# Sums of two matmuls side by side in 27 steps of two halves instead of 28

## The chip, the cores and the metric

The kernel runs on one NeuronCore of a Trainium2 chip. The metric is the device time of one execution in microseconds (us). The engines are TensorE (PE, with its weight loads as PEld), VectorE (DVE), ScalarE (ACT), GpSimd (POOL) and SyncE (SP); here nearly all transfers are issued from SP's queue.

## The reference

A transformer block on `x` of 2048 rows and 576 columns, all float32. Six vectors `sa, ca, ga, sb, cb, gb` come from `silu(c) @ w_mod`.

```python
h = layernorm(x) * (1 + ca) + sa
q, k, v = split(h @ wqkv)                 # 32 heads of 18
p = softmax(q @ k.T * 18 ** -0.5)
x = x + ga * ((p @ v) @ wo)
h = layernorm(x) * (1 + cb) + sb
x = x + gb * (silu(h @ w1) @ w2)          # w1: 576 x 4608, w2: 4608 x 576
```

## The kernel before

To keep float32 accuracy with a rounded matmul type, most operands are split into a high and a low part, and a product is the sum of high x high, high x low and low x high. The 576 columns are four tiles of 128 and a fifth of 64. `PASS` lists 14 passes of a sum: three for each of the four full tiles, and two for the fifth. The fifth tile has its 64 columns twice: rows 0 to 63 hold the high part of the activation, rows 64 to 127 its low part, and the weights stand on both halves alike. So one pass with the high weights gives high x high and low x high, and a second with the low weights gives high x low and, on the lower half, low x low.

Work comes in quads of four heads by a block of 512 queries: four blocks of eight quads. A quad has a stage of score maxima (`psa`, L674, reduced by DVE at L676), then the exponential scores (`psb`, L731, ACT at L733) and the value sums (`psv`, L768, four matmuls of 32 columns for each key tile). The maxima of a finished quad are negated and split into `ms` (`max_a`), transposed (`pst`), copied to `mt` (`max_copy`), and written by four small transfers (`max_rows`, L710) into spare rows of the queries `qt`; the exponential scores of that quad need them.

When the eight quads of a block are done, `post` queues its output projection (`proj`, `psp`), layernorm, transpositions (`o_T`, `h_T`) and the feed-forward network (`mlp1`, the first layer, and `mlp2`) as pieces of a filler, which are spread between the score steps of the next block. What is left after the fourth block runs alone: the tail (`state["tail"]`). `Pair` carries out two sums at once. Outside the tail it works in halves of 64 rows: in one step one matmul on rows 0 to 63 and one on rows 64 to 127 run side by side for the two sums, which change places half way, at step 14:

```python
for h in (1, 0) if late else (0, 1):
    g = 1 - h if late else h
```

A pair of 14 passes is thus 28 steps. `GR` and `GP` cut these steps into parts for the filler. In the tail a step is one matmul on all 128 rows.

PE runs in the order in which the program issues. That order is set by a planner (`Plan`, `Filler`), which adds up costs of parts (`MMC`, `MMH`) and chooses at each turn between a score step ("half"), a run of value sums ("values") and a piece of filler ("half", or "full" for transpositions and other matmuls of 128 rows). The other engines' queues are ordered by a scheduler from the program's dependencies and buffers.

During the first block's projection and network the weights are converted (`weights`): a half of a tile is loaded into a staging buffer `raw` (three buffers), POOL multiplies it by the gate where there is one (L826), copies the high part (L827) and subtracts for the low part (L828), and the tile is stored for the later blocks (L829).

Of the kernel before, what the change touches and what calls it, by code (L numbers as in the profile page):

```python
# [18 lines left out]
P = 128  # L19
# [42 lines left out]
PB = 7  # L62
QKB = 3
GS = 2
GR = [range(i, min(i + GS, 28)) for i in range(0, 28, GS)]
NG = len(GR)
GQ = (range(0, 4), range(4, 8), range(8, 11), range(11, 14))
G2 = [range(i, i + 3) for i in range(0, 24, 3)]
GP = [range(i, i + 2) for i in range(0, 28, 2)]
MMC = 231  # L70
MMH = 133

# [260 lines left out]
def tile_adaln_block(ctx: ExitStack, tc: tile.TileContext, x, wqkv, wo, w1, w2, c, wfirst, wcol, out):  # L333
# [114 lines left out]
    class Pair:  # L448
# [3 lines left out]

        def __init__(self, ps, ops, n, halves, planned=True):
            self.ps, self.ops, self.n, self.halves, self.planned = ps, ops, n, halves, planned
            if planned:
                self.release = [plan.take("f") for _ in ps]

        def step(self, s):  # L460
            late, i = divmod(s, self.n)
            if not self.halves:
                lhsT, rhs = self.ops(late, i)
                mm(self.ps[late], lhsT=lhsT, rhs=rhs, start=(i == 0), stop=(i == self.n - 1))  # L464
                return
            for h in (1, 0) if late else (0, 1):
                g = 1 - h if late else h
                lhsT, rhs = self.ops(g, i)
                rows = slice(64 * h, 64 * h + 64)
                done = mm(self.ps[g], lhsT=lhsT[rows], rhs=rhs[rows], start=(s == 0), stop=(s == 2 * self.n - 1))  # L470
                if h == 1 and s == self.n - 1:
                    self.last = done
                    if self.planned:
                        self.change()
                        half["at"] = None
                        plan.op("A", plan.t + 200, 20, lambda t: half.update(at=t + TR))
                elif h == 1 and s == self.n:
                    tc.add_manual_dep(done.ins, self.turn.ins.name, SYNC, reason="the other halves' writes to this bank")
# [208 lines left out]
            later.append((now + MB, 3, 110, lambda: max_b(t), lambda: t.get("ms_at")))  # L687

    def max_a(t):
        negm = at1.tile([P, 4, NST], F32, name="negm", bufs=2)  # L690
        nc.vector.tensor_reduce(negm, t["mx"], axis=AX.X, op=ALU.max, negate=True)
        ms = at1.tile([P, 2, 4, NST], F32R, name="ms", bufs=2)
        nc.vector.tensor_copy(ms[:, 0], negm)
        nc.vector.tensor_sub(ms[:, 1], negm, f(ms[:, 0]))
        t["ms"] = ms
        chain([("V", 230), ("V", 180), ("V", 180)], plan.t, None, lambda at: t.update(ms_at=at + TR))
# [4 lines left out]
        return ps  # L701

    def max_copy(t, ps):
        t["mt"] = at1.tile([32, P], F32R, name="mt", bufs=2)
        nc.vector.tensor_copy(t["mt"], ps[:32, :P])

    def max_rows(t):
# [69 lines left out]
    def out_b(i, ov):  # L777
        b, qd = divmod(i, NQUAD)
        ps = aux([P, NST, P], "pso")
        for s4 in range(NST):  # L780
            nc.tensor.transpose(ps[:, s4, :], ov[:, s4 * P:(s4 + 1) * P], ident)  # L781
        rec = att.tile([P, NST, 4], F32, name="rec", bufs=2)
        psr = ps.rearrange("p s (h c) -> p s h c", h=4)
        nc.vector.reciprocal(rec, psr[:, :, :, DH])
        if qd == 0:
            if b:
                fill.until("h_T")
            o[b] = att.tile([P, NST, 640], F32, tag="o", name="ot", bufs=1)
        for s4 in range(NST):
            nc.vector.tensor_mul(o[b][:, s4, 72 * qd:72 * qd + 72].rearrange("p (h c) -> p h c", h=4), psr[:, s4, :, :DH],  # L790
                                 rec[:, s4, :, None].to_broadcast([P, 4, DH]))
        rel = plan.take("a")
        chain([("V", 260)] + [("V", 225)] * 4, plan.t + 100, None, rel)
        del quads[i]
        if qd == NQUAD - 1:
            nc.gpsimd.tensor_copy(o[b][:, :, D:640], o[b][:, :, 512:D])
            post(b)
# [18 lines left out]
    def weights(w, src, scr, first, gate=None):  # L816

        if not first:
            nc.sync.dma_start(f(w), f(scr))
            return  # L820
        n = w.shape[2] // 2
        for cs in (slice(0, n), slice(n, 2 * n)):
            raw = mp["p"].tile([P, 320], F32, tag="raw", name="raw", bufs=3)[:, :n]
            nc.sync.dma_start(raw, src[:, cs])
            if gate is not None:
                nc.gpsimd.tensor_tensor(raw, raw, gate[:, cs], op=ALU.mult)  # L826
            nc.gpsimd.tensor_copy(w[:, 1, cs], raw)  # L827
            nc.gpsimd.tensor_tensor(w[:, 0, cs], raw, f(w[:, 1, cs]), op=ALU.subtract)  # L828
        nc.sync.dma_start(f(scr), f(w))  # L829
# [16 lines left out]
    def post(b):  # L846
# [7 lines left out]

        def o_T(kt):
            if kt == 0:
                c["th"] = pool.tile([P, KT, QB], F32R, tag="th", name="th")
                c["tl"] = pool.tile([P, 4, QB], F32R, tag="tl", name="tl")
            ps = bank("psT", psF)
            for j in range(NST):  # L860
                nc.tensor.transpose(ps[:, j * P:(j + 1) * P], ob[:, j, kt * P:(kt + 1) * P], ident)
            hi = c["th"][:, kt, :]
            chain([("A", 600), ("V", 690)], plan.t, None, plan.take("f"))
            nc.scalar.activation(hi, ps, AF.Copy)
            if kt < 4:
                nc.vector.tensor_sub(c["tl"][:, kt, :], ps, f(hi))
            else:
                nc.vector.tensor_sub(hi[64:], ps[64:], f(hi)[64:])

        def proj(j, part):  # L870
            if part == 0:
                def ops(g, i):
                    kt, a, w = PASS[i]
                    return (c["tl"] if a else c["th"])[:, kt, j * P:(j + 1) * P], c["wo", kt][:, 1 - w, g * HH:(g + 1) * HH]

                c["pp"] = Pair([bank("psp", psA)[:, :HH] for _ in range(2)], ops, 14, not state["tail"])
            for s in GP[part]:
                c["pp"].step(s)
            if part == len(GP) - 1:
                for g in range(2):  # L880
                    add_x1(j, g, c["pp"].ps[g])
                    plan.op("AV"[g == 0], plan.t + 200, 440, c["pp"].release[g])
# [19 lines left out]

        def h_T(kt):
            if kt == 0:
                c["hh"] = pool.tile([P, KT, QB], F32R, tag="th", name="hh")
                c["hl"] = pool.tile([P, 4, QB], F32R, tag="tl", name="hl")
            ps = bank("psT", psF)
            chain([("A", 780), ("V", 430)], plan.t, plan.take("f"))
            for j in range(NST):
                nc.tensor.transpose(ps[:, j * P:(j + 1) * P], ob[:, j, kt * P:(kt + 1) * P], ident)  # L910
            tmp, hi = etmp(), c["hh"][:, kt, :]
            mod_out(ps, kt, 1, tmp)
            mod_hi(hi, tmp)
            mod_lo(kt, hi, c["hl"][:, kt, :] if kt < 4 else None, tmp, nc.vector if last and kt % 2 == 0 else nc.gpsimd)

        def rest(n):
# [44 lines left out]
        def mlp1(i, part):  # L961
            if part == 0:
                def ops(g, k):
                    kt, a, w = PASS[k]
                    return c["w1", i + g][:, 1 - w, kt * P:(kt + 1) * P], (c["hl"] if a else c["hh"])[:, kt, :]

                c["p1"] = Pair([bank("ps1", psA) for _ in range(2)], ops, 14, not state["tail"])
            for s in GR[part]:
                c["p1"].step(s)
            if part < NG - 1:  # L970
                return
            us = c["p1"].ps
            if not state["tail"]:

                us = [etmp(), etmp()]
                nc.scalar.activation(us[0], c["p1"].ps[0], AF.Copy)
                nc.vector.tensor_copy(us[1], c["p1"].ps[1])
                for n in range(2):
                    chain([(("A", 600), ("V", 690))[n], ("A", 630), ("V", 690), ("A", 630)], plan.t + 200, c["p1"].release[n])
            for g_ in range(2):  # L980
                u, t = us[g_], etmp()
                nc.scalar.activation(t, u, AF.Tanh, scale=0.5)  # L982
                nc.vector.scalar_tensor_tensor(t, t, 1.0, u, op0=ALU.add, op1=ALU.mult)  # L983
                g = pool.tile([P, 2, QB], F32R, tag="g", name="g", bufs=GB)
                nc.scalar.activation(g[:, 0, :], t, AF.Copy)  # L985
                (nc.vector if last else nc.gpsimd).tensor_tensor(g[:, 1, :], t, f(g[:, 0, :]), op=ALU.subtract)  # L986
                c["g", i + g_] = g
# [565 lines left out]
```

## Time and profile before

| | |
|---|---|
| median of 3 runs | 2488.92 us (2485.57 to 2490.62) |
| profiled execution | 2492.01 us, span 2490.2 us |
| granted TensorE clock | 0.996 |
| busy: PE, DVE, ACT, POOL | 96%, 72%, 60%, 23% |
| first-layer matmuls of 64 rows, on `hh` and on `hl` | 2160 and 864 records, some missing |
| projection matmuls of 64 rows, on `th` and on `tl` | 480 and 192 |

A row of the timeline gives start, length, engine, line, operation, output and inputs, and a count; in brackets stands how long the engine was idle before it and what ended that. L470 is `Pair`'s matmul in halves, L464 the one on all rows. A matmul's length includes its way through the array, so matmuls that follow each other overlap in the records; what one costs is read from start to start.

### The profile page before, as it was taken

Reading aid. Unit: us, or ns where it says so; the run is one execution under the profiler, and the core shown is the slowest. Engines: PE = TensorE matmul, PEld = TensorE weight load, DVE = VectorE, ACT = ScalarE, POOL = GpSimd, SP = SyncE. Lnnn points to the kernel's source line nnn. Section 1 sums busy time; section 2 is a strip of 40 time slices with the busy share of each in tenths; the row PEclk is TensorE's granted clock in tenths of the full one; section 3 lists DMA queues with packets and bytes.
Section 4 is the critical chain, followed back from the end, with each engine's and each line's share of the span. In section 5 each row is a group of like instructions: output and inputs, shape, how many; then the busy total and the mean of one; then the engine's idle time right before and its main releaser. Section 6 shows DMA issues by size and latency. Waiting matters only on the chain.

```text
span 2490.2 us, 51321 instructions
## 1 busy us (share of the span) xinstructions
PE 2399.7 (96%) x20192; PEld 1574.5 (63%) x20192; DVE 1787.7 (72%) x3180; ACT 1490.4 (60%) x2712; POOL 577.9 (23%) x729
## 2 busy tenths in 40 slices
PE   5999999998999999999999999999999999999999
PEld 4874344433556666666666666666666666678988
DVE  7868788887877777777877777778777777334333
ACT  4237667766666766666666666666666666742121
POOL 4100000012566566652211111111211111110000
PEclk9999999999999999999999999999999999999999
DMA  6843333343455555553543433332633343226563
GB/s 234 269 133 110 110 108 110 110 146 106 137 180 184 169 181 179 199 168 123 172 146 128 144 125 127 131 134 95 209 127 121 127 160 118 103 101 239 172 221 120
DMA packets 159394, 372.02 MB, mean 149 GB/s; under 512 B 17754, under 2 KB 55034, under 8 KB 159154
## 3 DMA queue, kind: packets, MB, share of 16 engines
q1 hardware_dynamic: 154562, 366.45, 44.1%
q8 instruction: 160, 2.62, 0.5%
q10 hardware_dynamic: 4592, 2.29, 0.3%
q14 instruction: 80, 0.66, 0.1%
HBM read 282.35 MB, written 85.80 MB: 148 GB/s over the span
## 4 chain that ended last, share of the span: by engine, by line
PE 86%; DVE 7%; DMA 2%; ACT 2%; POOL 1%; issue 1%; SPq 1%; ACTq 0%; DVEq 0%; POOLq 0%
PE ps L470 26%; PE psv L768 19%; PE psa L674 14%; PE ps L464 10%; PE psb L731 8%; DVE mx L676 4%; PE psqk L551 3%; PE psp L470 1%; PE psv L470 1%; PE pso L781 1%; DVE etmp L983 1%; DMA xt<-in_x 1%; PE psp L464 1%; ACT pt L733 1%; ACT etmp L982 1%
## 5 line engine op out<-in xcount | busy, mean ns | idle before, releaser
L676 DVE TENSOR_REDUCE mx<-psa 128x1 f32<-128x512 f32 x2048 | 1345.4, 687 | 372.5 <-PE psb L731 250.1
L733 ACT ACTIVATE pt<-psb 128x512 f32<-128x512 f32 x2048 | 1163.1, 598 | 562.2 <-PE psb L731 393.3
L674 PE MATMUL psa<-kt,qt 54*128 54x512 f32 x2048 | 770.4, 424 | 26.9 <-DVE mx L676 22.7
L731 PE MATMUL psb<-qt,kt 56*128 56x512 f32 x2048 | 787.8, 428 | 8.5 <-DMA qt<-mt 5.1
L674 PEld LDWEIGHTS psa<-kt,qt 54*128 54x128 f32 x2048 | 345.6, 185 | 418.2 <-DVE mx L676 279.7
L768 PE MATMUL psv<-pt,vt 128*32 128x512 f32 x4096 | 534.7, 605 | 0.0
L470 PE MATMUL ps<-w2t,g 64*128 64x288 f32 x4992 | 417.5, 294 | 0.1
L470 PEld LDWEIGHTS ps<-w2t,g 64*128 64x128 f32 x4992 | 387.0, 186 | 35.2 <-issue 10.6
L470 PE MATMUL ps<-hh,w1t 64*128 64x512 f32 x2160 | 384.6, 395 | 1.7 <-POOL hh L405 1.6
L731 PEld LDWEIGHTS psb<-qt,kt 56*128 56x128 f32 x2048 | 347.3, 185 | 39.1 <-ACT pt L733 18.4
L470 PEld LDWEIGHTS ps<-hh,w1t 64*128 64x128 f32 x2160 | 219.8, 186 | 60.5 <-issue 10.6
L986 POOL TENSOR_TENSOR g<-etmp,g 128x512 fp32r<-128x512 f32 x108 | 138.3, 1297 | 405.4 <-ACT g L985 345.4
L891 POOL TENSOR_TENSOR x<-x,gt 128x288 f32<-128x288 f32 x116 | 92.8, 800 | 489.1 <-ACT gt L890 479.1
L768 PEld LDWEIGHTS psv<-pt,vt 128*32 128x32 f32 x4096 | 93.6, 108 | 177.7 <-issue 169.2
L470 PE MATMUL ps<-hl,w1t 64*128 64x512 f32 x864 | 185.7, 393 | 1.0 <-POOL hl L403 1.0
L887 DVE TENSOR_TENSOR x<-ps,x 128x288 f32<-128x288 f32 x184 | 84.0, 457 | 122.6 <-PE ps L464 71.5
L464 PE MATMUL ps<-w2t,g 128*128 128x288 f32 x960 | 130.6, 295 | 1.7 <-ACT g L985 0.9
L464 PEld LDWEIGHTS ps<-w2t,g 128*128 128x128 f32 x960 | 128.6, 188 | 3.3 <-ACT g L985 1.2
L982 ACT ACTIVATE eq<-ps 128x512 f32<-128x512 f32 x36 | 21.6, 599 | 146.3 <-PE ps L464 146.3
L464 PE MATMUL ps<-hh,w1t 128*128 128x512 f32 x360 | 106.8, 390 | 0.5 <-DVE hh L405 0.5
L529 POOL TENSOR_TENSOR wql<-raw,wqh 128x640 fp32r<-128x640 f32 x13 | 20.7, 1589 | 372.6 <-PE psa L674 112.0
L470 PEld LDWEIGHTS ps<-hl,w1t 64*128 64x128 f32 x864 | 93.0, 186 | 18.5 <-POOL hl L403 2.8
(140 smaller groups left out, 2084.7 us busy)
## 6 DMA issues: line engine op xcount, KB each, us to landing
w1t<-w1s SPq DMA_DIRECT2D x108, 640.0 KB
w2t<-w2s SPq DMA_DIRECT2D x108, 576.0 KB
kt<-kscr SPq DMA_DIRECT2D x512, 108.0 KB
w1s<-w1t SPq DMA_DIRECT2D x36, 640.0 KB
w2s<-w2t SPq DMA_DIRECT2D x36, 576.0 KB
vt<-vscr SPq DMA_DIRECT2D x32, 608.0 KB
qt<-qscr SPq DMA_DIRECT2D x128, 108.0 KB
raw<-in_w SPq DMA_DIRECT2D x72, 160.0 KB
```

The costliest lines, as they stand in the source:

```text
L464: mm(self.ps[late], lhsT=lhsT, rhs=rhs, start=(i == 0), stop=(i == self.n - 1))
L470: done = mm(self.ps[g], lhsT=lhsT[rows], rhs=rhs[rows], start=(s == 0), stop=(s == 2 * self.n - 1))
L551: mm(qk_ps[0], lhsT=w[b][:, kt, :], rhs=(hTl if a else hTh)[:, kt, n * 512:(n + 1) * 512], start=(i == 0), stop=(i == 13))
L674: mm(ps, lhsT=t["q"][64 * j:64 * j + 54, hp, stt * P:(stt + 1) * P], rhs=t["k", kc, hp][64 * j:64 * j + 54, :], start=True, stop=True)
L676: return lambda: nc.vector.tensor_reduce(t["mx"][:, 2 * j + hp, stt, kc:kc + 1], ps, axis=AX.X, op=ALU.max)
L731: mm(ps, lhsT=t["k", kt // 4, hp][64 * e:64 * e + 56, kt % 4 * P:(kt % 4 + 1) * P], rhs=t["q"][64 * e:64 * e + 56, hp, :], start=True, sto ...
L733: nc.scalar.activation(t["P"][kt, hp][:, e, :], ps, AF.Exp, scale=SCALE)
L768: mm(t["ps"][32 * h:32 * h + 32, :], lhsT=t["v"][:, c0:c0 + 32], rhs=t["P"][kt, h // 2][:, h % 2, :], start=(kt == 0), stop=(kt == NKT - 1 ...
L887: nc.vector.tensor_add(c["x1"][j][:, hs], ps, c["x1"][j][:, hs])
L891: nc.gpsimd.tensor_add(c["x1"][j][:, hs], c["x1"][j][:, hs], t)
L982: nc.scalar.activation(t, u, AF.Tanh, scale=0.5)
L986: (nc.vector if last else nc.gpsimd).tensor_tensor(g[:, 1, :], t, f(g[:, 0, :]), op=ALU.subtract)
```

## The change

The low x low product is left out. The high part of the fifth tile is copied by ACT to rows 64 to 127 of an extra column block (index `KT`) of `th` and `hh`. The second sum's high x low product of the fifth tile then runs on these rows at step 13, beside the first sum's; step 27 falls away for both sums. This holds for `proj` and `mlp1` outside the tail. `GP` and `GR` have 14 parts as before, the last one of one step, and the planner is given the smaller cost. The copies are also made in the tail, where nothing reads them. For the space of the extra columns, `raw` has two buffers instead of three, and `negm`, `ms`, `mt` and `rec` one instead of two.

```diff
-GR = [range(i, min(i + GS, 28)) for i in range(0, 28, GS)]
+GR = [range(i, min(i + GS, 27)) for i in range(0, 27, GS)]
-GP = [range(i, i + 2) for i in range(0, 28, 2)]
+GP = [range(i, min(i + 2, 27)) for i in range(0, 27, 2)]
...
+        def half(self, g, h, i):
+            if self.extra and g == 1 and h == 1 and i == self.n - 1:
+                lhsT, rhs = self.extra()
+            else:
+                lhsT, rhs = self.ops(g, i)
+            rows = slice(64 * h, 64 * h + 64)
+            return lhsT[rows], rhs[rows]
...
+            end = 2 * self.n - (2 if self.extra else 1)
             for h in (1, 0) if late else (0, 1):
                 g = 1 - h if late else h
-                lhsT, rhs = self.ops(g, i)
-                rows = slice(64 * h, 64 * h + 64)
-                done = mm(self.ps[g], lhsT=lhsT[rows], rhs=rhs[rows], start=(s == 0), stop=(s == 2 * self.n - 1))
+                lhsT, rhs = self.half(g, h, i)
+                done = mm(self.ps[g], lhsT=lhsT, rhs=rhs, start=(s == 0), stop=(s == end))
...
-        negm = at1.tile([P, 4, NST], F32, name="negm", bufs=2)
+        negm = at1.tile([P, 4, NST], F32, name="negm", bufs=1)
-        ms = at1.tile([P, 2, 4, NST], F32R, name="ms", bufs=2)
+        ms = at1.tile([P, 2, 4, NST], F32R, name="ms", bufs=1)
-        t["mt"] = at1.tile([32, P], F32R, name="mt", bufs=2)
+        t["mt"] = at1.tile([32, P], F32R, name="mt", bufs=1)
-        rec = att.tile([P, NST, 4], F32, name="rec", bufs=2)
+        rec = att.tile([P, NST, 4], F32, name="rec", bufs=1)
-            raw = mp["p"].tile([P, 320], F32, tag="raw", name="raw", bufs=3)[:, :n]
+            raw = mp["p"].tile([P, 320], F32, tag="raw", name="raw", bufs=2)[:, :n]
...
-                c["th"] = pool.tile([P, KT, QB], F32R, tag="th", name="th")
+                c["th"] = pool.tile([P, KT + 1, QB], F32R, tag="th", name="th")
+                nc.scalar.activation(c["th"][64:, KT, :], ps[64:], AF.Copy)
                 nc.vector.tensor_sub(hi[64:], ps[64:], f(hi)[64:])
...
+                def extra():
+                    return c["th"][:, KT, j * P:(j + 1) * P], c["wo", 4][:, 0, HH:2 * HH]
-            for s in GP[part]:
+            for s in range(28)[2 * part:2 * part + 2] if state["tail"] else GP[part]:
...
-                c["hh"] = pool.tile([P, KT, QB], F32R, tag="th", name="hh")
+                c["hh"] = pool.tile([P, KT + 1, QB], F32R, tag="th", name="hh")
+            if kt == 4:
+                nc.scalar.activation(c["hh"][64:, KT, :], tmp[64:], AF.Copy)
...
+                def extra():
+                    return c["w1", i + 1][:, 0, 4 * P:5 * P], c["hh"][:, KT, :]
-            for s in GR[part]:
+            for s in range(28)[GS * part:GS * part + GS] if state["tail"] else GR[part]:
```

Three places show how the change moves instructions. Up to the first projection the order on PE is the same in both kernels.

The first is on PE, the second half of the first projection pair. `wo` with a number is a tile of the weights, 6314 the fifth; two matmuls make a step. First the kernel before, then the changed one:

```order
L470 MATMUL psp<-wo_6290,th 128x288 x4
L470 MATMUL psp<-wo_6290,tl 128x288 x2
L470 MATMUL psp<-wo_6302,th 128x288 x2
L674 MATMUL psa<-kt_86,qt 128x512
L731 MATMUL psb<-qt,kt_90 128x512
L470 MATMUL psp<-wo_6302,th 128x288 x2
L470 MATMUL psp<-wo_6302,tl 128x288 x2
L470 MATMUL psp<-wo_6314,th 128x288 x4
```

```order
L480 MATMUL psp<-wo_6290,th 128x288 x4
L480 MATMUL psp<-wo_6290,tl 128x288 x2
L480 MATMUL psp<-wo_6302,th 128x288 x4
L480 MATMUL psp<-wo_6302,tl 128x288 x2
L480 MATMUL psp<-wo_6314,th 128x288 x2
L684 MATMUL psa<-kt_86,qt 128x512
L741 MATMUL psb<-qt,kt_90 128x512
```

The fifth tile has one step instead of two, and the score step in between has moved behind the pair.

The second is on PE in the last block of attention, where the outputs of a finished quad are transposed (`pso`). Before, then changed:

```order
L470 MATMUL ps_25030<-w2t,g 128x288
L470 MATMUL ps_25031<-w2t,g 128x288
L781 MATMUL pso<-ident,ov 128x128 x4
L768 MATMUL psv_25116<-pt_2108,vt_2109 32x512 x2
L768 MATMUL psv_25116<-pt_2102,vt_2109 32x512 x2
L768 MATMUL psv_25116<-pt_2103,vt_2109 32x512 x2
L768 MATMUL psv_25116<-pt_2104,vt_2109 32x512 x2
L674 MATMUL psa<-kt_88,qt 128x512
```

```order
L778 MATMUL psv_24873<-pt_2105,vt_2109 32x512 x2
L778 MATMUL psv_24873<-pt_2106,vt_2109 32x512 x2
L684 MATMUL psa<-kt_89,qt 128x512
L741 MATMUL psb<-qt,kt_92 128x512
L684 MATMUL psa<-kt_89,qt 128x512
L741 MATMUL psb<-qt,kt_93 128x512
L791 MATMUL pso<-ident,ov 128x128 x4
L480 MATMUL ps_25012<-w2t,g 128x288
L480 MATMUL ps_25013<-w2t,g 128x288
```

Before, the transposition was followed by a run of value sums; now score steps stand between the value run and the transposition, and steps in halves follow it.

The third is on SP in the first block's network, ahead of the maxima's transfers of a quad (`qt<-mt`). `raw` loads bring weights, `w1s` and `w2s` store them. Before, then changed:

```order
L829 DMA w1s<-w1t 128x1280
L824 DMA raw<-in_w 128x288
L648 DMA kt_87<-kscr 54x512
L824 DMA raw<-in_w 128x288
L829 DMA w1s<-w1t 128x1280
L824 DMA raw<-in_w 128x288
L710 DMA qt<-mt 1x8x128 x4
```

```order
L658 DMA kt_87<-kscr 54x512
L839 DMA w2s<-w2t 128x1152
L834 DMA raw<-in_w 128x320 x2
L839 DMA w1s<-w1t 128x1280
L834 DMA raw<-in_w 128x320
L834 DMA raw<-in_w 128x288
L720 DMA qt<-mt 1x8x128 x4
```

Other weights stand ahead of the maxima's transfers than before, and the key load has moved ahead of them.

More of the change, by code (lines that the diff above doesn't have):

```diff
@@ L448, in tile_adaln_block, with __init__ @@
     class Pair:
-        def __init__(self, ps, ops, n, halves, planned=True):
-            self.ps, self.ops, self.n, self.halves, self.planned = ps, ops, n, halves, planned
+        def __init__(self, ps, ops, n, halves, planned=True, extra=None):
+            self.ps, self.ops, self.n, self.halves, self.planned, self.extra = ps, ops, n, halves, planned, extra
             if planned:
                 self.release = [plan.take("f") for _ in ps]
+        def half(self, g, h, i):
[5 more added lines that the diff above has]
+            return lhsT[rows], rhs[rows]
         def step(self, s):
@@ L874, in ops @@
                     return (c["tl"] if a else c["th"])[:, kt, j * P:(j + 1) * P], c["wo", kt][:, 1 - w, g * HH:(g + 1) * HH]
-                c["pp"] = Pair([bank("psp", psA)[:, :HH] for _ in range(2)], ops, 14, not state["tail"])
-            for s in GP[part]:
+                def extra():
+                    return c["th"][:, KT, j * P:(j + 1) * P], c["wo", 4][:, 0, HH:2 * HH]
+                c["pp"] = Pair([bank("psp", psA)[:, :HH] for _ in range(2)], ops, 14, not state["tail"], extra=None if state["tail"] else extra)
+            for s in range(28)[2 * part:2 * part + 2] if state["tail"] else GP[part]:
                 c["pp"].step(s)
@@ L965, in ops @@
                     return c["w1", i + g][:, 1 - w, kt * P:(kt + 1) * P], (c["hl"] if a else c["hh"])[:, kt, :]
-                c["p1"] = Pair([bank("ps1", psA) for _ in range(2)], ops, 14, not state["tail"])
-            for s in GR[part]:
+                def extra():
+                    return c["w1", i + 1][:, 0, 4 * P:5 * P], c["hh"][:, KT, :]
+                c["p1"] = Pair([bank("ps1", psA) for _ in range(2)], ops, 14, not state["tail"], extra=None if state["tail"] else extra)
+            for s in range(28)[GS * part:GS * part + GS] if state["tail"] else GR[part]:
                 c["p1"].step(s)
```

## The prediction

> **What bounds the kernel now.** I read the page's busy shares and chain first, then busy time by stage, then what TensorE waits for while the feed-forward network runs, and last the timeline of TensorE there. The stage rows give start and end, length, and busy time (instructions) of PE, PEld, DVE, ACT and POOL, then granted clock, DMA share and GB/s. The stages are cut at the first transposition after each attention block (562 us is just before the first one's end).
>
> ```profile
> PE 2399.7 (96%) x20192; PEld 1574.5 (63%) x20192; DVE 1787.7 (72%) x3180; ACT 1490.4 (60%) x2712; POOL 577.9 (23%) x729
> PE 86%; DVE 7%; DMA 2%; ACT 2%; POOL 1%; issue 1%; SPq 1%; ACTq 0%; DVEq 0%; POOLq 0%
> ...
> 562.00:657.00 95.00, 81.60 (x631) 40.40 (x626) 77.19 (x154) 58.30 (x105) 25.86 (x44) 0.98 0.30 94
> 657.00:1214.00 557.00, 540.93 (x5098) 357.49 (x5098) 427.43 (x730) 368.18 (x665) 313.95 (x433) 1.00 0.53 171
> 1214.00:1752.00 538.00, 532.42 (x5092) 355.91 (x5090) 415.98 (x726) 365.42 (x661) 88.20 (x90) 1.00 0.41 138
> 1752.00:2249.00 497.00, 492.11 (x4542) 335.11 (x4541) 321.68 (x574) 318.92 (x583) 82.57 (x82) 1.00 0.38 131
> ```
>
> From 657 to 2249 us TensorE is busy for 1565.5 of 1592 us (98%) at full clock, and 86% of the chain is its own work. A busy share can hide waits under overlapping matmuls, so the waits of PE's own queue in that stretch (total us, times, longest):
>
> ```profile
> PE psa L674 <- DVE mx L676: 8.0, 15, 1.0
> PE psb L731 <- DMA qt<-mt: 3.9, 1, 3.9
> PE pst L700 <- DVE mx L676: 2.8, 5, 0.6
> ```
>
> The largest is 8.0 us in 1592. So there a step of TensorE that is left out should come off the end, unless something else takes its place. Now the price of a step, of a run of value sums (L768), and of going in and out of it, from the timeline of PE (start, length, line, operation, count):
>
> ```profile
> 1402.80 0.39 PE L674 MATMUL psa<-kt,qt 54*128 54x512 f32 x1
> ...
> 1403.12 0.28 PE L700 MATMUL pst<-ident,ms 128*32 128x128 f32 x1
> 1403.33 0.73 PE L470 MATMUL ps<-hh,w1t 64*128 64x512 f32 x4
> 1403.90 0.39 PE L470 MATMUL ps<-hl,w1t 64*128 64x512 f32 x2
> ...
> 1405.75 0.39 PE L674 MATMUL psa<-kt,qt 54*128 54x512 f32 x1
> ...
> 1406.07 1.07 PE L768 MATMUL psv<-pt,vt 128*32 128x512 f32 x8
> 1407.07 0.49 PE L674 MATMUL psa<-kt,qt 54*128 54x512 f32 x1
> ...
> 1407.41 0.62 PE L470 MATMUL ps<-hh,w1t 64*128 64x512 f32 x4
> ...
> 1411.37 0.63 PE L470 MATMUL ps<-hh,w1t 64*128 64x512 f32 x4
> 1411.93 1.92 PE L768 MATMUL psv<-pt,vt 128*32 128x512 f32 x16
> 1413.79 0.50 PE L674 MATMUL psa<-kt,qt 54*128 54x512 f32 x1
> ```
>
> Lengths overlap, so I take starts. Between 1407.41 and 1411.37 stand 17 steps of two halves (first-layer and score steps cost alike): 3.96 / 17 = 0.233 us a step. A value run of one key tile (x8) takes 1.00 us to the next start, of two (x16) 1.86: 0.86 a tile and 0.14 fixed. Going in costs 1406.07 - 1405.75 = 0.32 against 0.233, +0.09; the first step after it 1407.41 - 1407.07 = 0.34, +0.11. A full-row transposition costs +0.09 on the way in (1403.12 - 1402.80 = 0.32) and +0.10 behind it (0.57 for two steps).
>
> **The change part by part.**
>
> Steps removed, the gain. A first-layer pair gives up one step of 0.233. Blocks one to three each have 18 such pairs, 54 x 0.233 = 12.6 us. The order of the instructions agrees: 108 first-layer matmuls fewer. A projection pair is shorter (288 columns):
>
> ```profile
> 1176.66 0.43 PE L470 MATMUL psp<-wo,th 64*128 64x288 f32 x4
> ...
> 1177.45 0.41 PE L731 MATMUL psb<-qt,kt 56*128 56x512 f32 x1
> ```
>
> Six steps lie between these starts, 0.79 / 6 = 0.132 us; 4 pairs in 3 blocks give 12 x 0.132 = 1.6 us. The fourth block (the tail) keeps 28 full-row steps. Together -14.2 us, all in the stretch where TensorE waits for next to nothing. The Trainium skill (TensorE: Matmul & The Clock Gate, Back-to-back issue gap) gives 216 ns between warm matmuls of 512 columns, N/2.4 + 2.5 ns. By that the two terms would be 54 x 0.216 + 12 x 0.1225 = 13.1 us, an estimate from the page; the trace's 0.233 decides.
>
> The new order, a loss. Costs of parts set the order that the planner writes for PE, so everything behind the first projection moves. I counted in the two orders how often PE changes its kind of work from there to the end of attention: half-row to values 269 before and 288 after, values to half-row 291 and 300, half-row to full 65 and 62, full to half-row 43 and 50, full to values 24 and 14; 293 value runs become 302. At the prices above: 19 x 0.09 = 1.7; 9 x (0.14 + 0.11) = 2.2; -3 x 0.09 = -0.3; 7 x 0.10 = 0.7; full to values no row above prices alone, so -10 x (0 to 0.10), I take 0.05 as the middle, -0.5. Sum +3.9 us. Bounds: 0, if these drains lie beside waits that would have been there anyway, to 4.4. I take 3.9, since the waits are so few.
>
> The new copies on ScalarE: 8, one in each projection's and one in each first layer's transpositions, 64 x 512. Nearest row, same columns:
>
> ```profile
> L864 ACT ACTIVATE th<-psT x20: 578/598/637, 603.7 to 2221.4; 128x512 fp32r<-128x512 f32 x20
> ...
> ACT pt L733 <- PE psb L731: 304.0, 418, 4.4
> ```
>
> Median 598 ns, so 4.8 us of ACT work in all. From 560 to 2220 us ACT stands idle 304 us waiting for scores from PE (second row), which covers it; I take 0. Without that cover each of the six before the tail would hold up the exponentials queued behind it by 0.6 us, and those hold up score banks: at most 3.6 us. The low end is 0, since a copy added can shorten nothing. The planner does not count these copies. In the tail ACT is idle for most of the time, 48.00 us busy of 241 by the stage row,
>
> ```profile
> 2249.00:2490.00 241.00, 233.61 (x1392) 211.48 (x1391) 89.80 (x158) 48.00 (x77) 3.03 (x4) 1.00 0.54 189
> ```
>
> so 0 there too. The waits for the half-way turn stay where they were (step 14).
>
> Maxima rings and the reciprocals' ring of one instead of two: the next write of such a tile now waits for the last reader of the quad before. The last of these readers, `qt<-mt`, must leave before the quad's exponential scores start, and the next write is a quad later (successive maxima):
>
> ```profile
> 850.77 0.22 DVE L691 TENSOR_REDUCE negm<-mx 128x16 f32<-128x64 f32 x1
> 917.16 0.22 DVE L691 TENSOR_REDUCE negm<-mx 128x16 f32<-128x64 f32 x1
> ```
>
> 66 us apart, so 0. Were a read ever that late, VectorE would stand with the score maxima queued behind it.
>
> Raw staging of two instead of three. This matters only while the first block converts weights (up to about 1150 us). A load into `raw` waits, on SP's queue, until POOL is done with the tile that had the buffer; behind it on SP stand key loads and the four small `qt<-mt` transfers, without which a quad's exponential scores cannot start. Even with three buffers this bit once:
>
> ```profile
> 717.73 0.77 SPq L648 DMA_DIRECT2D kt<-kscr  x1
> 723.45 0.33 SPq L824 DMA_DIRECT2D raw<-in_w  x1
> 725.04 0.32 SPq L829 DMA_DIRECT2D w1s<-w1t  x1
> 725.46 0.38 SPq L824 DMA_DIRECT2D raw<-in_w  x1
> 725.93 2.84 SPq L710 DMA_DIRECT2D qt<-mt  x4
> ...
> 719.62 0.27 DVE L705 CAST mt<-pst 32x128 fp32r<-32x128 f32 x1
> ...
> 722.16 0.44 POOL L827 CAST w1t<-raw 128x320 fp32r<-128x320 f32 x1
> 722.57 0.86 POOL L828 TENSOR_TENSOR w1t<-raw,w1t 128x320 fp32r<-128x320 f32 x1
> ...
> 730.06 0.47 PE L731 MATMUL psb<-qt,kt 56*128 56x512 f32 x1 [3.89 <-DMA qt<-mt]
> ```
>
> The maxima were ready at 719.9 (719.62 + 0.27). SP had stood since 718.5 before a `raw` load that went out at 723.45, when POOL's subtraction at 722.57 had freed its buffer; the maxima left at 725.93, and PE stood 3.89 us. That is one of the eight quads that meet such a queue. With two buffers each load waits on a nearer reader, so the same can strike more often: bounds 0 (the scheduler that orders SP has pushed loads apart, and no PE row names a late weight) and 8 x 3.9 = 31 us. I take half a stall more, 2 us, nearest to the one in eight that the trace shows. That the weights themselves come late I take as 0: POOL is busy 313.95 of 557 us in that stage.
>
> Sum: -14.2 + 3.9 + 2 = -8.3 us. The profiled execution took 2492.0 (span 2490.2), which gives 2483.7. It lies 3.1 us above the median of the runs, 2488.9, so against the median 2480.6: I say 2481.
>
> **The rivals.**
>
> *VectorE becomes the bound, about 2489.* Each score bank is released by a maximum on DVE. In 562 to 657 us DVE is 81% busy (77.19 of 95) and PE only 86%; in the blocks behind, DVE is at 77% (427.43 of 557; 415.98 of 538). Taking 4.7 us of PE work out of a block raises that to 78%. If PE waits for banks by what it saves, the block keeps its length and the time is that of before. Against it: of all PE waits in these blocks only 8.0 us were for these maxima. The Trainium skill (TensorEngine Tiling (Array Packing), PSUM Bottleneck) says that tiling speeds TensorE and not the emptying of PSUM, which may then bind; by that rule this rival would hold, and the trace's 8.0 us speak against it so far.
>
> *SP's queue makes it slower, 2494 or more.* Place: `qt<-mt` behind `raw` loads in the first block. With -14.2 + 3.9 the change has 10.3 us to lose; four stalls of 3.9 more (15.6 us) put it 5.3 above, 2494.2; all eight quads 2510. It decides from four further stalls on. For it: the row at 730.06, and the new order has six transfers of weights just ahead of `qt<-mt` at that quad. Against: seven of eight quads went free.
>
> *The changes of mode cost nothing, 2475.* If the extra value runs stand where PE would have waited anyway, and no stall comes, the whole 14.2 arrives: 2488.9 - 14.2 = 2474.7. Against it are the dense starts above. That the step is not really left out is no rival: the order has 132 matmuls fewer.
>
> **How the numbers follow.** Forecast (2477 to 2485) 0.60, VectorE 0.14, SP's queue slower 0.12, whole gain 0.14. About 5 us, 0.2% of 2488.9, is what a measurement of this kernel can tell from no change; so faster means below 2483.9 and slower above 2493.9. The forecast gives 0.53 to faster and 0.07 to the same, the whole gain 0.13 and 0.01, VectorE 0.14 to the same, SP's queue 0.12 to slower: 0.66, 0.22, 0.12. The range 2474 to 2493 takes in the whole gain and the return to before, and leaves out the stalls; within the likeliest case it is 2477 to 2485.
>
> **What would show it.** Right: the first two full blocks (557 and 538 us between first-layer transpositions) become shorter by 3 to 5 us each, the third too, and the tail stays at 241; PE's first-layer rows at 64 rows number 108 fewer with unchanged length; PE's busy share in the blocks stays near 98%. The mode term is right if a value run of one tile still takes 1.00 us. The staging term shows in `psb <- DMA qt<-mt` between 600 and 1150 us: about 4 to 8 us. VectorE as bound would show in `psa <- DVE mx` growing from 8 to 20 us or more. Wrong it would be made most easily by the new order itself: waits in places that neither the order nor this trace names.

## The result and the profile after

The changed kernel took 2527.84 us (median of 4 runs, 2520.34 to 2530.64), against 2488.8 for the kernel before: 39 us slower by the medians, and 36 by the ratio, 1.0144 [1.0124, 1.0163]. I had said 2481, with 2474 to 2493 as the range: the sign was wrong, and the time lies 35 us above the range. The profiled execution took 2530.64, its span 2528.8. The ratios further below leave out two executions with a much lower clock (2883 us at 0.75 with four staging buffers, which is the one that was profiled, and 2535 us at 0.91 of the kernel before).

The page of the changed kernel, its busy shares and its chain by engine:

```profile
PE 2406.2 (95%) x20060; PEld 1572.0 (62%) x20060; DVE 1786.8 (71%) x3180; ACT 1494.0 (59%) x2720; POOL 582.3 (23%) x729
PE 73%; DMA 8%; DVE 8%; POOL 5%; ACT 2%; issue 2%; SPq 1%; ACTq 0%; POOLq 0%; DVEq 0%
```

PE has 132 matmuls fewer, as announced, and yet 6.5 us more busy time. Its share of the chain fell from 86% to 73%; DMA rose from 2% to 8% and POOL from 1% to 5%. So matmuls became longer, and something with transfers and GpSimd came onto the path.

Where it lies is shown by a cut at the first transposition of each attention block's output (`th`, the row of 64 partitions on DVE): three blocks, then the tail. Columns as in the stage rows above. First before, then after:

```profile
608.00:1154.00 546.00, 527.38 (x4886) 343.50 (x4882) 420.13 (x717) 361.54 (x653) 321.50 (x446) 0.99 0.52 169
1154.00:1693.00 539.00, 533.24 (x5094) 355.69 (x5090) 416.04 (x726) 364.69 (x661) 88.23 (x90) 1.00 0.41 138
1693.00:2222.00 529.00, 522.51 (x4972) 349.47 (x4968) 355.41 (x631) 354.12 (x646) 87.43 (x90) 1.00 0.38 128
2222.00:2490.00 268.00, 260.04 (x1588) 237.68 (x1588) 105.54 (x205) 48.00 (x77) 6.91 (x11) 1.00 0.52 180
```

```profile
607.00:1191.00 584.00, 536.42 (x4842) 348.38 (x4838) 419.97 (x718) 361.77 (x655) 320.79 (x442) 0.96 0.48 157
1191.00:1739.00 548.00, 539.94 (x5112) 356.81 (x5109) 424.46 (x738) 373.07 (x677) 92.31 (x94) 1.00 0.41 138
1739.00:2258.00 519.00, 511.20 (x4861) 340.31 (x4860) 346.79 (x618) 347.77 (x635) 87.23 (x89) 1.00 0.38 130
2258.00:2528.00 270.00, 261.95 (x1588) 239.40 (x1588) 105.41 (x205) 49.39 (x80) 7.48 (x12) 0.99 0.51 179
```

Nearly the whole loss is in the first block, the only one that converts weights: 584 us instead of 546; the tail is 2 us longer. The second and third together are 1 us shorter (1067 against 1068; the new order moves some score work across their border, so they are read together). What PE waited for in the first block, before and then after (total us, times, longest):

```profile
PE psa L674 <- DVE mx L676: 5.9, 9, 1.0
PE psb L731 <- DMA qt<-mt: 3.9, 1, 3.9
```

```profile
PE psb L741 <- DMA qt<-mt: 23.4, 5, 8.9
PE psa L684 <- DVE mx L686: 11.2, 15, 1.9
PE psb L741 <- ACT pt L743: 8.3, 4, 3.8
```

It is the wait on the transposed maxima that the prediction named, and it grew to six times its size: three waits of 6.2 to 8.9 us and two under 1 us.

### The profile page after: what moved, and what is told of

The parts are those of the page before. It is cut to its first block, busy times and chain, and to the rows that moved or that the text cites. A ratio compares the mean times of both kernels' runs of the same rounds, so it can differ in the third digit from the quotient of the medians.

```text
span 2528.8 us, 51079 instructions
## 1 busy us (share of the span) xinstructions
PE 2406.2 (95%) x20060; PEld 1572.0 (62%) x20060; DVE 1786.8 (71%) x3180; ACT 1494.0 (59%) x2720; POOL 582.3 (23%) x729
## 4 chain that ended last, share of the span: by engine, by line
PE 73%; DMA 8%; DVE 8%; POOL 5%; ACT 2%; issue 2%; SPq 1%; ACTq 0%; POOLq 0%; DVEq 0%
PE ps L480 21%; PE psv L778 16%; PE psa L684 12%; PE ps L474 9%; PE psb L741 7%; DMA raw<-in_w 6%; DVE mx L686 4%; PE psqk L561 3%; PE psp L480 2%; PE psv L480 1%; POOL w1t L838 1%; POOL w2t L838 1%; POOL raw L836 1%; DVE etmp L1002 1%; POOL g L1005 1%
## 5 line engine op out<-in xcount | busy, mean ns | idle before, releaser
L480 PE MATMUL ps<-hh,w1t 64*128 64x512 f32 x2052 | 370.0, 395 | 1.6 <-POOL hh L405 1.2
L480 PEld LDWEIGHTS ps<-hh,w1t 64*128 64x128 f32 x2052 | 208.6, 186 | 48.0 <-issue 3.5
```

What stands on the lines that cost most here:

```text
L480: done = mm(self.ps[g], lhsT=lhsT, rhs=rhs, start=(s == 0), stop=(s == end))
```

## Experiments

All are compared with the kernel before on the same chip. "Block one" is the first stretch of the cut above. "Raw" is the number of staging buffers.

| kernel | time, us | ratio to before | block one, us |
|---|---|---|---|
| before, raw 2 | 2535.89 | 1.0179 [1.0157, 1.0202] | 586 |
| before, four small rings of one | 2489.53 | 0.9992 [0.9981, 1.0002] | 547 |
| changed, raw 3 | 2479.33 | 0.9949 [0.9933, 0.9965] | 538 |
| the same, PE in the order of before | 2475.13 | 0.9939 [0.9926, 0.9952] | 544 |
| the same, 28 steps | 2489.50 | 0.9994 [0.9985, 1.0002] | 546 |
| changed, maxima sent from ACT | 2588.44 | 1.0383 [1.0364, 1.0402] | 592 |
| changed, raw loads from POOL | 2592.49 | 1.0406 [1.0391, 1.0421] | 647 |
| before, raw 4 | 2486.53 | 0.9985 [0.9977, 0.9994] | not read |
| before, raw 1 | 2745.24 | 1.1025 [1.0992, 1.1058] | 789 |
| changed, maxima 3 us earlier | 2516.42 | 1.0106 [1.0081, 1.0130] | 575 |
| changed, raw in quarters | 2516.90 | 1.0109 [1.0077, 1.0141] | 576 |
| 26 steps, PE in the order of before | 2460.30 | 0.9890 [0.9876, 0.9904] | 536 |

**One part alone: the staging ring.** The kernel before, with

```diff
-            raw = ... name="raw", bufs=3
+            raw = ... name="raw", bufs=2
```

> The kernel before with one edit: raw staging of two buffers instead of three; 28 steps, all other rings as they were. Theory 1 (the staging ring holds up SP's queue in the first block, so that qt<-mt is late and TensorE stands): 2515 to 2540 us, the first block between output transpositions (544 us in the kernel before) at 575 to 590, waits psb<-DMA qt<-mt there of 15 to 30 us and a granted clock under 0.98 in that block. Theory 2 (the shifted order of PE that comes with 27 steps makes the waits): 2489 within 5 us, as before. Theory 3 (the small rings of one or the added copies): 2489 within 5 us.

2535.89 us: the ring alone costs 1.79%, 44 us, more than the whole change lost. Its first block and PE's largest waits there:

```profile
606.00:1192.00 586.00, 543.83 (x4886) 355.66 (x4882) 421.40 (x718) 362.55 (x654) 321.03 (x441) 0.96 0.48 156
```

```profile
PE psb L731 <- DMA qt<-mt: 24.8, 5, 10.0
PE psa L674 <- DVE mx L676: 6.5, 11, 1.5
PE ps L470 <- POOL w2t L827: 3.3, 1, 3.3
```

PE carries out the same matmuls as before (x4886 in both), so the 40 us can be split. Idle time rose from 546 - 527.38 = 18.6 to 586 - 543.83 = 42.2, by 23.6; of that 20.9 are the maxima's waits (24.8 - 3.9). The other 16.4 us are busy time: the same matmuls took longer, at a granted clock of 0.96 instead of 0.99. With the ring alone the exponentials make PE wait for 1.0 us only.

**One part alone: the rings of the maxima and the reciprocals.** `negm`, `ms`, `mt`, `rec` with one buffer in the kernel before.

> The kernel before with one edit: negm, ms, mt and rec have one buffer instead of two; raw three, 28 steps. Theories 1 and 2: 2489 within 5 us, since the next write of such a tile comes a quad (66 us) later. Theory 3 (a write waits for a late reader): 2500 us or more, with VectorE waiting for qt<-mt or for pst.

2489.53, no difference.

**The change without its staging ring.** Raw 3 again; the space comes from the ring of score maxima (`mx`, 2 to 1) and from small layernorm tiles.

```diff
-            raw = ... name="raw", bufs=2
+            raw = ... name="raw", bufs=3
-        t["mx"] = ... bufs=2
+        t["mx"] = ... bufs=1
```

> The changed kernel with raw staging of three buffers again; the space comes from mx, of one buffer instead of two, and from the small tiles of the second layernorm (statistics, reciprocal root), of one. 27 steps, copies and rings of one stay. Theory 1: the loss goes, 2478 to 2486 us, first block between output transpositions at 540 to 545, psb<-DMA qt<-mt under 8 us. Theory 2: 2515 to 2535 as in the changed kernel. Theory 3: as theory 2.

2479.33, faster than both kernels, with PE's order the same as in the changed kernel. So against it the changed kernel shows what two buffers do, matmul for matmul (x4842 in both):

```profile
601.00:1139.00 538.00, 523.11 (x4842) 340.00 (x4838) 421.67 (x717) 361.12 (x656) 323.19 (x446) 1.00 0.52 171
```

```profile
PE psa L684 <- DVE mx L686: 9.5, 14, 1.5
PE psb L741 <- DMA qt<-mt: 2.9, 2, 2.0
```

584 - 538 = 46 us: 536.4 - 523.1 = 13.3 of longer matmuls and 32.7 of idle time. Of the idle time 20.5 is the maxima (23.4 - 2.9), 8.1 the exponentials (`pt`, 8.3 against 0.2) and 2.6 the weights themselves.

**The order of PE, and the step itself.** To the last kernel, the costs that the planner had before:

```diff
-                fl.add(MMH * len(GP[part]), ...
+                fl.add(MMH * 2, ...
-                fl.add(MMC * len(GR[part]), ...
+                fl.add(MMC * GS, ...
```

PE then has exactly the order of before less 132 matmuls.

> The previous experiment (27 steps, raw three) with the planner's costs of the filler's parts as in the kernel before: the last part of a pair is one step but is counted as two, so the order on TensorE is that of the kernel before with 132 matmuls taken out, and the changes of mode are as before (378 half-row to values instead of 397). If the 19 further changes of mode with their drains cost the 3.9 us of the prediction, it is 3 to 5 us faster than the previous experiment: ratio to before 0.9925 to 0.9940 (14.2 us saved, about 2476). If they lie beside waits anyway, it is the same within 2 us: 0.9945 to 0.9955.

2475.13, the best that computes everything. The other way round, 28 steps with all copies, wide tiles and rings of one kept, is the price of what the change adds:

> The kernel of 27 steps and raw three with the step put back: 28 steps and the order on TensorE of the kernel before, but with the eight copies on ScalarE, the wider th and hh, and the rings of one. If copies and rings cost nothing: as before, ratio 0.998 to 1.002. If the six copies before the tail hold up exponentials: 1.001 to 1.0015 at most (3.6 us). A loss beyond that would mean the rings of one cost.

2489.50, no difference: copies and small rings cost nothing. Between these two, which differ in the 132 matmuls alone, the medians lie 14.4 us apart but the profiled spans only 8.7 (2486.4 and 2477.7). So I left out one more step, the high x low product of the fifth tile for both sums; that kernel lacks a product that the result needs and only measures the price.

> The best kernel so far (27 steps, three raw buffers, the costs of before, so that PE keeps the order of before) with one more step left out of each pair outside the tail: the last product of the fifth tile for both sums is not computed. The order on PE is the same less 108 first-layer and 24 projection matmuls. It measures the price of a step once more, since the profiles of the kernels with 28 and 27 steps in this order lie only 8.7 us apart while their medians lie 14.4 apart. Theory 1 (the price read from starts holds, 0.233 and 0.132 us a step): another 14.2 us, 2475.1 - 14.2 = 2461 us, ratio to before about 0.988. Rival (PE has other waits behind the steps, and a step brings only the 8.7 us of the profiles): 2475.1 - 8.7 = 2466 us or, counted from before, 2489 - 17.4 = 2472, ratio 0.991 to 0.993.

2460.30, ratio 0.9890: two steps give 27.4 us (24 to 31 by the interval) where 28.4 was worked out and the rival said 17.4. The price from the starts holds. The 8.7 of one pair of profiles falls short mostly in the first block, which became about 1.6 us shorter where the starts give 4.7. Its clock differed (0.99 with 28 steps, 0.98 with 27, 1.00 with 26): by the estimate described further below, the profiled execution with 27 steps lost 9.6 us of work to the clock there, and the one with 28 steps 4.6.

**Another queue for the maxima, or for the raw loads.** In the changed kernel:

```diff
-            nc.sync.dma_start(f(t["q"]...), f(t["mt"]...))
+            nc.scalar.dma_start(f(t["q"]...), f(t["mt"]...))
```

> The changed kernel with one edit: the four transfers qt<-mt of each quad are issued from ScalarE's queue instead of SP's, so they no longer stand behind raw loads; raw two, 27 steps. Theory 1: the waits psb<-DMA qt<-mt of 24.6 us shrink to under 8 and the clock of the first block rises again, 2495 to 2510 us; key loads still stand behind raw on SP, and ScalarE pays its issue time, 4 x 0.6 us a quad. Theory 2: 2520 to 2535, as the changed kernel. If ScalarE's issuing delays the exponentials, 2 us a quad are lost, up to 60 us.

A miss: 2588.44. The wait on `qt<-mt` is gone from PE's list, but ACT now stands before the transfers with its exponentials behind them. PE's wait, then ACT's own, over the whole execution:

```profile
PE psb L741 <- ACT pt L743: 58.4, 30, 9.9
```

```profile
ACT pt L743 <- DMA qt<-mt: 76.1, 19, 11.9
```

This happens in every block, not only in the one that loads weights (block two 563 us, block three 533). The loads of `raw` from POOL instead:

```diff
-            nc.sync.dma_start(raw, src[:, cs])
+            nc.gpsimd.dma_start(raw, src[:, cs])
```

> The changed kernel (raw two, 27 steps) with the raw loads issued from POOL's own queue instead of SP's. POOL frees the buffers itself, so SP no longer waits for them except for the stores. Theory 1 as to place (the loss is SP's queue held up): psb<-DMA qt<-mt falls from 24.6 us to under 8, the first block between output transpositions from 583.8 to 540 to 565 us, the whole 2480 to 2510; POOL pays about 1 us of issuing for each of 154 loads, which it has room for. Rival (the loss is that two buffers make the weights late on POOL, whichever queue loads them): the waits for w1t and w2t grow and the time stays at 2520 or above.

A second miss: 2592.49. The page gives the loads 4.2 us from issue to landing. In block one POOL waits 144.6 us for them, less than the 181.7 in the changed kernel, but issuing 142 of them takes it 78.8 us more, 0.56 each. PE now waits for POOL's GELU products (`g`) as well. The maxima are still late. They stand on SP behind the stores of converted weights, which wait for POOL: 421 us in block one, against 135 in the changed kernel. The page's row of the loads, then PE's waits and one of SP's, over the whole execution:

```profile
raw<-in_w POOLq DMA_DIRECT2D x72, 160.0 KB, 4.2
```

```profile
PE ps L480 <- POOL g L1005: 31.8, 7, 13.8
...
PE psb L741 <- DMA qt<-mt: 22.0, 5, 7.8
```

```profile
SPq L839 <- POOL w2t L838: 222.0, 35, 8.8
```

So a queue that waits makes its followers late here too; how much of the loss is POOL's own issuing, this run does not separate.

**The dose.** Four buffers, then one, in the kernel before. For four the space came from the small rings as above.

> The kernel before (28 steps, no copies) with raw staging of four buffers; the space comes from rings of one for negm, ms, mt, rec, mx and the second layernorm's small tiles. Theory 1 (SP stands before a raw load until POOL has freed its buffer, and what is behind it is late): the one stall of 3.9 us at three buffers goes as well, and key loads come earlier: 2 to 6 us faster, ratio 0.9975 to 0.9993. Rival (three buffers already cover POOL and the landing): the same, 0.999 to 1.001.

> The kernel before with a single buffer for the raw weights (raw 3 to 1), nothing else. The dose so far: four buffers 2486.5, three 2489, two 2536. Theory 1 (what counts is the round trip of a half: GpSimd converts it, the buffer comes free, SyncE issues the next load, it lands, GpSimd starts): with one buffer nothing overlaps, so a half takes GpSimd's 1.33 us (W1) or 2.04 us (W2) plus some 2.8 us from release to landing, 72 x 4.1 + 72 x 4.8 = about 640 us for a block's weights, more than the 546 us that a block has before. Block 1 then follows the weights: 680 to 760 us with the rest of GpSimd's work, and the whole 2620 to 2720 us, PE waiting mostly for GpSimd's W1 and W2 tiles. Rival (each buffer taken away costs the same, since each only makes the late transposed maxima later by one step): 2536 + 46 = about 2580 us, with psb <- DMA qt<-mt as the largest wait.

2486.53 and 2745.24. The loss is far from even: three to four gave 4 us, three to two cost 44, two to one 211 more. For a single buffer I had the size too low (2620 to 2720) and the kind half right: PE's waits in block one are 82.2 us for converted tiles, as I had said, but 81.1 us for the maxima, which the rival had named. POOL's waits for landed weights in block one, with three buffers, two and one:

```profile
POOL raw L826 <- DMA raw<-in_w: 56.9, 41, 5.0
POOL w1t L827 <- DMA raw<-in_w: 33.2, 20, 4.4
```

```profile
POOL raw L826 <- DMA raw<-in_w: 97.7, 61, 4.9
POOL w1t L827 <- DMA raw<-in_w: 79.9, 39, 5.1
```

```profile
POOL raw L826 <- DMA raw<-in_w: 195.8, 66, 5.4
POOL w1t L827 <- DMA raw<-in_w: 189.1, 63, 4.6
```

90.1, 177.6 and 384.9 us for 144 halves. With one buffer 129 halves wait 3.0 us each, the trip from release over issue to landing (for example 2.34 us, from POOL's last read at 800.87 to its next start at 803.21); with three, 61 halves still wait at all.

**How it reaches PE.** In the changed kernel, the transposed maxima made about 3 us earlier (`MB = 4` to `1`), the same instructions at another place:

> The changed kernel (two raw buffers) with the transposed maxima made and sent some three half slots (about 3 us) earlier (MB 4 to 1); the same instructions, another place in the order. Theory 1a (the bulk of the loss is the late load of the transposed maxima behind raw loads on SyncE, which stood 4 to 11 us behind its cast): 3 us of head start cut the five stalls of 23.4 us to about 10, and with them the drop of the clock: 2500 to 2515 us. Rival 1b (the loss is GpSimd's rate with two buffers, weights late, and the stall on the maxima is only where it shows): the load waits as long as before, or another wait takes its place: 2520 to 2535 us, no change.

2516.42, just outside the first theory's 2500 to 2515 and below its rival's 2520. The maxima's stalls fell from 23.4 to 14.9 us, not to 10: at the worst quad the cast ended 5 us earlier, but SP reached the transfers only 3.6 us earlier. Then the weights in quarters, four small buffers in the space of two:

> The changed kernel with the raw weights in quarters (128x160, four buffers in the same bytes as two of 128x320), each loaded and converted by itself; 144 more loads for SyncE and twice as many, half as long, conversions for GpSimd in a block. Theory A (the number of buffers in flight decides, so that GpSimd always has a landed one): stalls go as with three buffers, 2480 to 2495 us. Theory B (the bytes in flight against the round trip decide, and each load costs SyncE 0.33 us of issue and GpSimd a fixed part of each conversion whatever its size): 2525 us or more, with GpSimd and SyncE both busier and PE waiting for W1 and W2 tiles or the maxima as before.

2516.90, between the two expectations, so neither theory holds whole. POOL waits less for weights, 117.5 us in place of 181.7, but the maxima stall PE longer (28.4 us, one stall of 15.9). But the conversions in quarters take POOL 374.6 us instead of 320.8, so it gains only some 10 us by both. So this run does not show whether what stands on SP ahead of the maxima counts for itself. The kernel with earlier maxima speaks for it, with 9 us less by the ratios, though the intervals of that kernel and the changed one just touch.

## Why the prediction was wrong

*The staging term failed, and it alone decides.* I took 2 us, "nearest to the one in eight that the trace shows", with 31 as the top; it measured 44 alone and 48 inside the change (2527.8 against 2479.3). Three things were wrong in the working. The first and the third can be seen at the quad that I had quoted from the trace before. SP, POOL and PE of the changed kernel there:

```profile
722.13 0.33 SPq L834 DMA_DIRECT2D raw<-in_w  x1
722.51 0.35 SPq L658 DMA_DIRECT2D kt<-kscr  x1
725.70 0.33 SPq L839 DMA_DIRECT2D w2s<-w2t  x1
726.07 2.37 SPq L834 DMA_DIRECT2D raw<-in_w  x2
731.89 0.33 SPq L839 DMA_DIRECT2D w1s<-w1t  x1
732.30 1.33 SPq L834 DMA_DIRECT2D raw<-in_w  x2
733.69 2.67 SPq L720 DMA_DIRECT2D qt<-mt  x4
...
730.12 0.91 POOL L837 CAST w1t<-raw 128x320 fp32r<-128x320 f32 x2 [2.85 <-DMA raw<-in_w]
731.00 1.67 POOL L838 TENSOR_TENSOR w1t<-raw,w1t 128x320 fp32r<-128x320 f32 x2
...
722.32 0.27 DVE L715 CAST mt<-pst 32x128 fp32r<-32x128 f32 x1
...
737.61 0.89 PE L741 MATMUL psb<-qt,kt 56*128 56x512 f32 x2 [8.87 <-DMA qt<-mt]
```

First, the length of a stall. I priced each at the 3.89 us seen with three buffers. But the maxima (cast at 722.3) stand behind several raw loads, and with two buffers each load waits for a conversion of a half that was itself waiting for its load (2.85 us at 730.12). They left at 733.69, 11 us after the cast, and PE stood 8.87 us. The trips add up; the stall was not an event with a fixed price. Secondly, the number: five of the quads of the block stalled PE, three of them for 6 us or more, where I carried forward one in eight.

Thirdly, the clock. The 25 us with the end of this wait, the 25 after, and three stretches of 2 us out of the first, in the changed kernel:

```profile
725.00:750.00 25.00, 16.13 (x160) 11.79 (x156) 11.07 (x18) 10.03 (x19) 11.26 (x17) 0.80 0.56 169
750.00:775.00 25.00, 24.70 (x206) 15.66 (x200) 18.99 (x33) 16.50 (x30) 15.05 (x23) 1.00 0.53 175
...
734.00:736.00 2.00, 0.00 (x0) 0.00 (x0) 0.00 (x0) 0.00 (x0) 0.15 (x1) 0.50 0.78 229
738.00:740.00 2.00, 2.00 (x16) 2.00 (x16) 0.69 (x1) 1.09 (x2) 0.73 (x1) 0.50 0.64 246
742.00:744.00 2.00, 2.00 (x21) 1.07 (x22) 1.23 (x3) 1.50 (x4) 1.56 (x2) 1.00 0.47 151
```

The clock fell to half while PE was still waiting, and stayed there for some 3.7 us behind the wait, to about 741.3. So of the 5 us of clock that the first row lacks, 0.20 x 25, only 1.9 us fell on work. As an estimate I add up, over stretches of 1 us, PE's busy time times the clock that is missing. In block one this gives 12.7 us in the changed kernel against 2.3 with raw 3, and 16.2 with the ring alone against 3.3 before. That is 10.4 of the 13.3 us of longer matmuls in the one split above, and 12.9 of the 16.4 in the other. I had counted idle time only.

The Trainium skill (TensorE: Matmul & The Clock Gate, Part 1: The HAM clock gate) has the clock at half rate after an idle window of some 3.4 us. The trace agrees in kind: 0.93 in the kernel before from 725 to 750 us, with its one wait of 3.89 us, is 3.5 us at half rate, and 0.80 here is 10. But a long wait is not the only way there. In the changed kernel the clock was 0.93 from 925 to 950 us, with no single wait over 2.3 us, and 0.86 from 700 to 725 us, where PE waited three times for 1.1 to 1.4 us within 5 us. With the ring alone it was at half for some 10 us from 652 us on, behind waits of at most 0.9 us. This took 4.9 of that kernel's 16.2 us, and what set it off stays open.

*"That the weights themselves come late I take as 0: POOL is busy 313.95 of 557 us"* was wrong by this way, though small on PE directly (2.6 us). POOL had time, but in these rows it takes its instructions in order and stands while a half is under way. Behind the waiting instruction stands the residual sum `x<-x,gt`, for which ACT's next `gt` waits, and behind that the exponentials:

```profile
926.21 0.79 POOL L836 TENSOR_TENSOR raw<-raw,gb 128x288 f32<-128x288 f32 x1 [3.97 <-DMA raw<-in_w]
926.96 1.54 POOL L905 TENSOR_TENSOR x<-x,gt 128x288 f32<-128x288 f32 x2
...
927.78 0.41 ACT L904 ACTIVATE gt<-ps 128x288 f32<-128x288 f32 x1 [3.80 <-POOL x L905]
...
928.73 0.52 PE L741 MATMUL psb<-qt,kt 56*128 56x512 f32 x1 [2.27 <-ACT pt L743]
```

This is the second way to PE. ACT waited so four times in block one, 12.1 us in all, and not once with raw 3; three of these waits stand just ahead of PE's three larger waits for exponentials, and so make up most of the 8.1 us in the split above.

*The rival "SP's queue makes it slower"* had the place, the main wait and the point from which it decides, and got 0.12. Its own upper price, 2510 with all eight quads, was 18 us too low: 3.9 us a stall, no clock, and no second way over POOL and ACT.

*The steps removed: right.* 14.2 us was worked out; at raw 3 and the order of before the kernel gains 15.2 (0.61% of 2489, 12 to 18), and two steps gain 27.4.

*The new order: left open.* I took 3.9 us. The two kernels that differ in it measured 2479.3 and 2475.1, a loss of 2.5 us by the ratios, but their intervals overlap. The price that goes into the term holds: in the changed kernel a value run of one tile takes 1451.38 - 1450.39 = 0.99 us to the next start (1.00 was expected).

```profile
1450.39 1.06 PE L778 MATMUL psv<-pt,vt 128*32 128x512 f32 x8
1451.38 0.50 PE L684 MATMUL psa<-kt,qt 54*128 54x512 f32 x1
```

*Copies and small rings at 0: right* (2489.5 twice). *VectorE as the bound: wrong.* The best kernel's wait for score maxima in the blocks is 8.2 us, against 8.0 before, with all the steps gone. By the rule of the Trainium skill (TensorEngine Tiling (Array Packing), PSUM Bottleneck) the emptying of PSUM may bind once tiling has made TensorE faster; no run here shows it, this row speaks against it:

```profile
PE psa L684 <- DVE mx L686: 8.2, 18, 0.8
```

Without its staging term the sum says -10.3 us, and the changed kernel with raw 3 measured -12.7 (-16.7 to -8.7). The mechanism of the gain was right; that the sum without the term lies inside this interval may be luck in part, since no run shows the order's 3.9 us in it. A side condition of the change, one buffer in a ring, took nearly four times as much back.

## What to carry to other kernels

Price a shorter ring by the loop that refills it (convert, release, issue, land) and by everything that stands in order behind the waiting instruction, on each queue of that loop; the stalls that the longer ring shows are no measure, since the third buffer was just what hid the rest. Add to the waits of TensorE the slower matmuls beside them; in the two splits here the longer matmuls came to 0.4 and 0.7 of the idle time added, and in the second a part belonged to no long wait. When space is short, take it from a ring that no such loop refills (`negm` is written every 66 us, and `mx` is written and read by VectorE alone, one after the other) and not from one that is refilled every few microseconds: the same 27 steps then gain 12.7 to 15.2 us instead of losing 36.

## What was not expected of the hardware

The granted clock in a 25 us window fell to 0.80 around one wait of 8.87 us, and was back at 1.00 in the next; it fell to 0.86 in a window whose longest wait was 1.36 us. With one staging buffer it was 0.85 over the whole of block one, where the same matmuls (x4886 before, x4882 there) took 586 us instead of 527. And a move to another issuing queue did not free the waiting transfer: it moved the wait to that engine's own work, 58.4 us of late exponentials for ACT.
